# Linear attention in an adaptive transformer block: the query side token-major, scaled in place and turned by DMA

## The chip, the cores and the metric

One Trainium2 chip, one core. The time is that of one execution on the device in microseconds, the median of three runs: 209.04 us before (208.19 to 209.4). The profiled execution of the same kernel spans 207.3 us from its first to its last instruction; times read from the profile count from its start. The granted TensorE clock is 1.000 over the whole span.

The engines are called PE (TensorE: matmuls, with PEld for its weight loads), DVE (VectorE), ACT (ScalarE), POOL (GpSimd) and SP (SyncE, which only issues transfers here). Each runs its own instructions in program order; semaphores order them between engines.

## The reference

Sequence 2,048 tokens, width 512, 32 heads of 16, hidden width 1,376, all in bfloat16. Cut to what matters:

```python
mod = (silu(c) @ w_mod)            # six rows of 512: sa, ca, ga, sb, cb, gb
h = layernorm(x) * (1 + ca) + sa
q, k, v = heads(h @ wqkv)          # 32 heads of 16
pq = q @ w_phi[head]; pk = k @ w_phi[head]
phi_q = concat([softmax(pq), softmax(-pq)])   # 32 features a head, no causal mask
phi_k = concat([softmax(pk), softmax(-pk)])
kv  = sum over tokens of phi_k x v            # 32 x 16 a head
z   = sum over tokens of phi_k                # 32 a head
o   = (phi_q @ kv) / (phi_q @ z + 1e-6)
x = x + ga * (o @ wo)
h = layernorm(x) * (1 + cb) + sb
out = x + gb * ((silu(h @ w_gate) * (h @ w_up)) @ w_down)
```

The numerator and the denominator of `o` hold the same `phi_q`. A factor that both signs of one head's `phi_q` share cancels in the quotient.

## The kernel before

Tokens are worked in 16 tiles of 128 (four chunks of four). The program is written as a list of operations with the buffers that each reads and writes. Some have more than one engine to choose from. A fixed list, `ORDER`, says in which order they are placed and on which engine, and a small timing model inside the kernel only decides which buffer each gets, how instructions are interleaved, and where TensorE would idle. There it puts matmuls of ones whose result nobody reads ("fillers", line 1046).

The key side, once for each token tile; `Wk2` is the key weight with `w_phi` folded in:

```python
def k_tile(i):
    # PE: pk = hT^T Wk2, v = hT^T Wv, four matmuls of 512 columns each
    # ACT: e = exp(+pk), exp(-pk)           (128 x 1024)
    # DVE: S = sum of e over 16 features    (64 sums a token)
    # DVE or ACT: R = 1 / S
    # POOL: phik = e * R
    # ACT or DVE: va = v, with a column of ones
def kv_tile(i):     # PE: 8 matmuls of 65 columns: kv_ps += phik^T va, for four heads and both signs each
    ...
```

The query side is feature-major: 128 features by 512 tokens. It keeps the bare exponentials of both signs and normalizes later:

```python
def q_front(c_i, j):
    for k in range(KD):
        nc.tensor.matmul(pq()[:], lhsT=Wq2[:, k, j * P:(j + 1) * P], rhs=hT[c_i][k][:], ...)
    for sg in range(2):
        nc.scalar.activation(eTs[c_i, sg, j][:], pq()[:], ACT.Exp, scale=(1.0 if sg == 0 else -1.0))
```

The attention of a tile takes eight matmuls, one for eight heads of one sign, with 128 + 16 columns: numerators, the sums of the exponentials, and the products with z. DVE then joins the signs:

```python
NDW = P + 16
def attend(n):
    nd = Buf("four", lambda slot: four_ps[0])          # four banks of PSUM, one buffer
    for j in range(KD):
        for sg in range(2):
            nc.tensor.matmul(nd()[:, j, sg * NDW:(sg + 1) * NDW], lhsT=eTs[c_i, sg, j][:, ts_],
                             rhs=KVZ[:, sg * KD + j, :], start=True, stop=True)
    # ACT or DVE: Ssw[sg] = sums of the other sign          (two copies)
    # DVE: U = (products with z) * Ssw ; den = U(+) + U(-) ; den = 1 / den
    # DVE: A[sg] = sums of the other sign / den             (two products)
    # DVE: o2[sg] = numerators[sg] * A[sg]                  (two products of 128 x 512)

def turn(n, on_pe):
    if on_pe:      # tiles 0 and 1: PE, 8 matmuls against the identity add the signs and turn; ACT copies
        ...
    else:          # POOL adds the two signs, a DMA transpose on SP turns the sum
        pl.op("POOL", ..., fn=lambda: nc.gpsimd.tensor_tensor(o()[:], o2()[:, 0]..., o2()[:, 1]..., op=ALU.add))
        pl.op("XBAR", ..., fn=lambda: nc.sync.dma_start(oT()[:], o()[:], transpose=True))
```

After it come `project` (four matmuls with `wo`, the residual, the statistics of the second normalization), the transposes of the normalized tile, and the feed-forward part: gate and up (`ffn_gu`, line 906), its last 96 features (`ffn_tail`, line 948), and down (line 978). The mask that places KV for the attention:

```python
for sg in range(2):
    for r in range(2):
        # DVE: KVZ block = kv_ps block * mask (64 partitions) ; KVZ z columns = (z + eps/2) * mask
```

First loads, all on one queue but the first two: x tiles 0 and 1 (256 KB), 2 and 3 (256), key weights (2 x 256), the first 1,024 columns of `w_mod` (4 x 256), value weights (512), x 4 to 7 (2 x 256), query weights (512), the rest of x (2 x 512). `w_phi` (16 KB) and `c` go on ACT's queue.

Of the kernel before, what the change touches and what calls it, by code (L numbers as in the profile page):

```python
# [30 lines left out]
NDW = P + 16  # L31
HG = 4 * DH
UNITS = [(0, 0, 1), (0, 1, 1), (0, 2, 1), (0, 3, 1), (1, 0, 2), (1, 2, 2), (2, 0, 2), (2, 2, 2), (3, 0, 2), (3, 2, 2)]


def fm_size(m):
# [4 lines left out]
QUOTA = {'q': 9, 'turn': 9, 'T': 9, 'T2': 9, 'wo': 9, 'down': 9, 'gu': 9, 'kv': 9, 'fold': 9}  # L41
# [4 lines left out]
EARLY = ("kv", "q", "fold", "T")  # L46
# [3 lines left out]
    28, 36, 0, 12, 76, 124, 4, 32, 16, 40, 8, 304, 316, 328, 340, 128, 60, 352, 80, 132, 136, 108, 92, 44, 48, 97, 64, 84, 356, 156, 160, 112, 68,  # L50
    116, 164, 168, 56, 73, 140, 144, 53, 176, 184, 172, 181, 120, 153, 150, 20, 24, 100, 105, 89, 216, 208, 220, 264, 212, 225, 256, 200, 192, 268,
    188, 452, 360, 444, 204, 260, 196, 472, 480, 364, 456, 376, 512, 273, 368, 228, 404, 276, 396, 388, 234, 412, 392, 448, 400, 408, 416, 476, 237,
    381, 504, 488, 282, 286, 288, 372, 484, 248, 240, 308, 420, 384, 424, 516, 252, 245, 636, 438, 430, 434, 320, 500, 332, 584, 492, 496, 508, 336,
    324, 312, 640, 460, 465, 520, 628, 592, 524, 612, 620, 616, 344, 348, 632, 624, 468, 680, 672, 596, 536, 528, 296, 293, 301, 588, 441, 540, 644,
    648, 548, 676, 544, 600, 604, 688, 532, 661, 654, 658, 666, 608, 685, 560, 704, 668, 700, 812, 692, 768, 732, 736, 740, 744, 708, 720, 976, 980,
    772, 776, 780, 804, 984, 988, 761, 749, 757, 712, 696, 753, 808, 817, 764, 884, 568, 724, 888, 916, 564, 717, 820, 892, 728, 832, 912, 948, 920,
    784, 824, 828, 900, 904, 1005, 997, 952, 908, 1001, 993, 1008, 1012, 1032, 1036, 924, 956, 932, 572, 936, 940, 897, 944, 1112, 960, 1144, 1176,
    1028, 1016, 1020, 964, 968, 928, 1060, 972, 1116, 1048, 1052, 1056, 1128, 1132, 1136, 556, 1024, 1140, 1040, 1216, 1180, 1148, 1192, 1196, 1200,
    1160, 1208, 1164, 1168, 1044, 576, 1212, 1240, 1244, 580, 1152, 1120, 1172, 1124, 788, 1184, 1224, 1228, 1157, 1204, 1236, 848, 1220, 1189, 1232,
    1304, 1308, 1316, 1312, 1324, 792, 796, 552, 856, 800, 1248, 1288, 1276, 1320, 1300, 852, 860, 1280, 1328, 868, 864, 1348, 1353, 1356, 1360, 1364,  # L60
    1368, 1372, 1076, 1252, 1084, 1100, 1284, 1080, 1292, 1104, 1256, 1088, 1520, 1296, 1376, 1525, 1528, 1532, 1536, 1540, 1544, 1260, 1108, 1264,
    1064, 1380, 1384, 1388, 1392, 1396, 1092, 1268, 1096, 1072, 1272, 1068, 872, 1688, 1692, 1332, 1548, 836, 1552, 880, 1400, 1696, 1700, 1556, 1406,
    1704, 844, 1708, 1712, 1416, 876, 840, 1420, 1408, 1860, 1413, 1428, 1464, 1716, 1560, 1864, 1564, 1424, 1868, 1568, 1872, 1432, 1876, 1436, 1880,
    1472, 1572, 1884, 1720, 1444, 1452, 1460, 1448, 1577, 1468, 1476, 1888, 1892, 1440, 1724, 1580, 2060, 1456, 1585, 1480, 2064, 1728, 2068, 2072,
    1732, 2076, 2080, 1496, 1736, 1588, 1500, 1484, 1592, 1488, 1628, 1636, 1612, 1740, 1746, 2084, 1748, 1492, 2032, 1620, 1648, 1596, 1652, 1504,
    2036, 2120, 1600, 2040, 2044, 1656, 2048, 1604, 2052, 1508, 1632, 1896, 2056, 1900, 1904, 1766, 1754, 1762, 2124, 1616, 1660, 2344, 2088, 1640,
    1757, 2128, 1800, 1804, 2348, 2352, 1908, 2356, 1512, 1516, 2132, 2360, 1624, 2364, 2092, 1912, 1918, 1920, 1812, 1784, 1792, 1608, 2368, 1644,
    1788, 1768, 1772, 1664, 2136, 2140, 1808, 1933, 1929, 1925, 2372, 1776, 1796, 2377, 2380, 2384, 1668, 2096, 1820, 1828, 1836, 2144, 1816, 1340,
    2388, 2392, 2396, 1672, 2400, 2100, 2104, 1824, 1937, 2149, 1780, 2432, 2108, 1832, 1840, 2656, 2661, 1956, 1964, 1940, 2664, 1676, 2404, 2112,
    2436, 2156, 1844, 2117, 1944, 1972, 1976, 2668, 2672, 2676, 1848, 1984, 2440, 1980, 1948, 2680, 2152, 2161, 2173, 1336, 2712, 2444, 2408, 1992,  # L70
    1960, 1952, 2170, 2166, 2000, 2684, 2192, 2412, 2448, 1988, 1968, 2208, 1996, 2716, 2008, 2196, 2688, 2416, 2452, 2200, 2692, 2420, 2696, 2424,
    2456, 2004, 2700, 2720, 2012, 2016, 2176, 2704, 2708, 2724, 2020, 2728, 2216, 2180, 2744, 2748, 2968, 2430, 2972, 2976, 2980, 2024, 2984, 2224,
    2732, 2461, 2204, 2736, 2988, 2184, 2228, 2236, 2464, 2244, 2264, 2212, 2252, 2232, 2992, 2188, 2468, 2240, 2996, 1852, 3024, 2260, 2272, 2268,
    2276, 2482, 2742, 2752, 2220, 3001, 3004, 3008, 3012, 3016, 2248, 2284, 2280, 2473, 2485, 2756, 3020, 2760, 3028, 2256, 2764, 2478, 3280, 3284,
    3288, 3292, 3296, 2288, 2296, 2292, 1856, 2320, 2488, 2324, 2328, 2776, 2504, 3300, 2768, 3056, 3060, 2300, 2304, 2773, 2492, 2028, 2496, 2508,
    3304, 3336, 3308, 3312, 2520, 2528, 2780, 2500, 2332, 2308, 3316, 2512, 3320, 3064, 3324, 3328, 3332, 2576, 2536, 2540, 3592, 3340, 3368, 2548,
    3068, 3072, 3076, 3080, 2544, 2552, 2556, 3032, 2786, 3597, 2797, 2584, 2794, 2564, 3600, 3604, 3608, 3612, 3036, 2336, 2790, 2572, 2560, 2592,
    2600, 3040, 2568, 2596, 3344, 3616, 2580, 3372, 3044, 2604, 3376, 3048, 3648, 1680, 3620, 2884, 3348, 3380, 2892, 2588, 2800, 2524, 3625, 3628,
    2532, 3352, 3632, 1684, 3652, 3086, 2832, 2836, 2804, 2888, 3356, 2808, 3092, 2812, 3384, 3636, 3052, 2840, 2896, 2900, 2312, 3088, 2516, 3640,
    2844, 2816, 2852, 3644, 2316, 2340, 2904, 2820, 2824, 2632, 2860, 2828, 3098, 2608, 2636, 3388, 3680, 3684, 3656, 3660, 3664, 3668, 2640, 2612,  # L80
    2616, 2620, 3109, 2912, 3105, 2848, 2856, 2868, 2908, 2644, 2872, 3688, 3672, 3677, 2876, 1345, 2916, 2864, 3360, 2880, 2944, 2948, 3692, 3696,
    3700, 2624, 3102, 3112, 3116, 3120, 3392, 2648, 3128, 3132, 3136, 3712, 3140, 2952, 2920, 3160, 3365, 3397, 3404, 2956, 3704, 3200, 2924, 3208,
    3709, 2961, 2964, 3124, 3400, 3180, 2928, 2932, 3168, 3188, 3144, 3184, 3164, 3216, 3172, 3192, 3152, 3224, 3148, 3220, 3228, 3422, 3196, 3716,
    3733, 3721, 3726, 3730, 3804, 3176, 3768, 2652, 2628, 3417, 3413, 3408, 3156, 3256, 3812, 3204, 3424, 3492, 3428, 3776, 3212, 3260, 3264, 3232,
    3500, 3752, 3432, 3808, 3236, 3268, 3756, 3760, 3764, 3736, 3740, 3744, 3788, 3240, 3816, 3784, 3512, 3244, 3440, 3792, 3520, 3436, 2936, 3796,
    2940, 3748, 3248, 3800, 3444, 3772, 3780, 3448, 3272, 3456, 3252, 3452, 3276, 3844, 3464, 3840, 3460, 3848, 3468, 3852, 3824, 3472, 3480, 3820,
    3476, 3528, 3832, 3828, 3836, 3484, 3856, 3880, 3536, 3884, 3496, 3504, 3488, 3508, 3888, 3892, 3516, 3524, 3860, 3864, 3532, 3544, 3896, 3900,
    3540, 3868, 3548, 3552, 3568, 3572, 3576, 3872, 3876, 3556, 3560, 3564, 3904, 3908, 3912, 3580, 3585, 3588, 3916, 3920,
# [27 lines left out]


class Op:
    def __init__(self, n, alts, preds, news, at):
        self.n, self.alts, self.preds, self.news, self.at = n, alts, preds, news, at  # L120
        self.end = None


class Plan:


    HOP = {"PE": 0.32, "DVE": 0.3, "ACT": 0.24, "POOL": 0.21, "SP": 0.0, "XBAR": 1.8, "NONE": 0.0}
    OWN = {"PE": 0.0, "DVE": 0.19, "ACT": 0.19, "POOL": 0.12, "SP": 0.0, "XBAR": 0.0, "NONE": 0.0}

    def __init__(self, slots, quota):  # L130
        self.ops = []
        self.slots, self.quota = slots, quota

    def op(self, alts, r=(), w=(), us=None, fn=None):
        if isinstance(alts, str):
            alts = [(alts, us, fn)]
        preds, news, at = set(), [], 0.0
        for b in r:
            preds.update(b.writers)
            at = max(at, b.at)  # L140
# [16 lines left out]
    def room(self, b, live):  # L157

        best = None
        for i in range(self.slots[b.tag]):  # L160
            if b.tag == "one" and not (b.kind == f"last{i - 4}" if str(b.kind)[:4] == "last" else i < 4 or b.kind in EARLY):
                continue
# [4 lines left out]
        if best is not None and b.kind in self.quota:  # L167
            busy = [x for x in live[b.tag].values() if x.kind == b.kind]
            over = len(busy) - self.quota[b.kind] + 1
            if over > 0:  # L170
                ends = [x.free_at() for x in busy]
                done = sorted(e for e in ends if e is not None)
                if len(done) < over:
                    return None
# [911 lines left out]
```

The softmax here doesn't subtract the row's maximum and nothing guards it: scores larger than these inputs give would overflow.

## Time and profile before

| | before |
|---|---|
| time, median of 3 | 209.04 us (208.19 to 209.4) |
| span of the profile | 207.3 us |
| first value projection on TensorE (line 617) | 13.36 us |
| last `kv_tile` ends | 56.7 us |
| first attention (line 781) | 59.32 us |
| first tail and gate/up matmuls (lines 948, 906) | 72.0 and 72.5 us |
| last matmul group (line 978) begins | 198.3 us |
| TensorE: attention, 128 matmuls of 144 columns | 16 groups of 0.50 us |
| DVE: reduce of a key tile, 128 x 1024 to 128 x 64 | 1,194 ns, 16 times |
| DVE: `o2`, 128 x 512 from PSUM | 683 ns, 32 times |
| POOL: add of the two signs | 1,154 ns, 14 times |
| SP: DMA transposes of 128 x 512 | 40, landing 2.4 us after issue |

A row of the profile's groups says line, engine, operation, output <- inputs, shapes, count, then busy time, mean time of one in ns, and the idle time before them with what ended it. The start of one matmul to the start of the next is shorter than its recorded length, as matmuls overlap; so the lengths on the chain are used for the pitch, not the means of the groups. The window tables give the busy time of each engine in a stretch of the span.

### The profile page before, as it was taken

How to read it: one execution, taken by the hardware profiler on the slowest of the kernel's cores; microseconds unless marked ns; L12 is line 12 of the kernel's file. 1: busy time of each engine (PE TensorE's matmuls, PEld its weight loads, DVE VectorE, ACT ScalarE, POOL GpSimd, SP SyncE). 2: the span in 40 equal slices, each digit the busy share in tenths (PEclk: the TensorE clock that was granted, in tenths of full speed). 3: DMA queues.
4: the chain of work that ended last, by engine and by line, in shares of the span. 5: the costliest groups of instructions: out<-in, count | busy, mean ns of one | idle time of the engine just before them, and what ended most of it. 6: DMA issues, size and time to landing. Idle time of an engine off the chain costs nothing.

```text
span 207.3 us, 4949 instructions
## 1 busy us (share of the span) xinstructions
PE 202.4 (98%) x1876; PEld 140.0 (68%) x1876; DVE 143.1 (69%) x351; ACT 114.0 (55%) x244; POOL 131.0 (63%) x172
## 2 busy tenths in 40 slices
PE   7999999999999999999999999999999999999994
PEld 2764656454555698785887876879675787698752
DVE  6699899999676886999789687887467222322232
ACT  2689999998789974335452542422532564044300
POOL 1069999899991546689678793677749254061451
PEclk9999999999999999999999999999999999999999
DMA  5996993797000011231611233202321330020012
GB/s 176 335 389 119 321 191 87 275 406 254 4 0 0 3 25 36 51 81 26 91 32 28 58 83 81 57 0 60 79 62 28 79 85 3 13 66 27 0 34 68
DMA packets 34025, 19.76 MB, mean 95 GB/s; under 512 B 25073, under 2 KB 30674, under 8 KB 34002
## 3 DMA queue, kind: packets, MB, share of 16 engines
q1 hardware_dynamic: 33712, 19.38, 33.5%
q8 instruction: 14, 0.23, 0.5%
q10 hardware_dynamic: 290, 0.08, 0.2%
q14 instruction: 9, 0.07, 0.1%
HBM read 11.58 MB, written 2.10 MB: 66 GB/s over the span
## 4 chain that ended last, share of the span: by engine, by line
PE 92%; DMA 2%; ACT 1%; POOL 1%; DVE 1%; SPq 0%; issue 0%; DVEq 0%
PE one_ps L906 34%; PE one_ps L978 18%; PE one_ps L852 7%; PE one_ps L613 6%; PE one_ps L673 6%; PE one_ps L617 5%; PE four_ps L781 4%; PE one_ps L948 3%; PE kv_ps L1046 2%; DMA wqkv_sb<-in_A_wqkv_dram 2%; PE kv_ps L649 2%; PE one_ps L447 1%; PE one_ps L551 1%; PE one_ps L540 1%; ACT e L624 1%; POOL phik L642 1%
## 5 line engine op out<-in xcount | busy, mean ns | idle before, releaser
L978 PE MATMUL one_ps<-wd_sb,gu 128*128 128x512 bf16 (+2 forms) x176 | 41.0, 372 | 0.0
L906 PE MATMUL one_ps<-hT,wg_sb 128*128 128x256 bf16 (+1 forms) x400 | 41.0, 251 | 0.0
L906 PE MATMUL one_ps<-hT,wu_sb 128*128 128x256 bf16 (+1 forms) x400 | 40.9, 251 | 0.0
L913 ACT ACTIVATE sg<-one_ps 128x512 bf16<-128x512 f32 (+1 forms) x42 | 23.7, 576 | 27.6 <-PE one_ps L906 26.4
L906 PEld LDWEIGHTS <-wg_sb 128*128 128x128 bf16 x400 | 32.7, 98 | 4.8
L906 PEld LDWEIGHTS <-wu_sb 128*128 128x128 bf16 x400 | 32.9, 98 | 4.2
L916 DVE TENSOR_TENSOR gu<-one_ps,sg 128x512 bf16<-128x512 f32 (+1 forms) x26 | 16.6, 640 | 22.1 <-PE one_ps L906 12.8
L642 POOL TENSOR_TENSOR phik<-e,R 128x1024 bf16<-128x1024 bf16 x16 | 30.5, 1930 | 1.1 <-ACT eT L679 0.7
L922 POOL TENSOR_TENSOR gu<-usb,sg 128x512 bf16<-128x512 bf16 x16 | 18.5, 1155 | 16.8 <-ACT sg L913 13.3
L978 PEld LDWEIGHTS <-gu 128*128 128x128 bf16 (+1 forms) x187 | 17.7, 98 | 15.0
L384 DVE BATCH_NORM_STATS2 st<-x_c 128x6 f32<-128x512 bf16 x32 | 21.3, 682 | 1.4 <-DMA x_c<-in_A_x_dram 1.1
L994 POOL TENSOR_TENSOR ot<-x_c,fg 128x512 bf16<-128x512 bf16 (+1 forms) x14 | 15.7, 1118 | 8.8 <-DVE fg L990 8.8
L839 POOL TENSOR_TENSOR o<-o 128x512 bf16<-128x512 bf16 x14 | 16.1, 1154 | 7.6 <-DVE o L819 7.1
L819 DVE TENSOR_TENSOR o<-four_ps,A 128x512 bf16<-128x512 f32 x32 | 20.5, 683 | 0.0
L634 DVE TENSOR_REDUCE S<-e 128x64 f32<-128x1024 bf16 x16 | 19.0, 1194 | 0.6 <-ACT e L624 0.4
L624 ACT ACTIVATE e<-one_ps 128x512 bf16<-128x512 f32 x32 | 17.7, 631 | 1.6 <-POOL phik L642 1.0
L990 DVE TENSOR_TENSOR fg<-one_ps,gab 128x512 bf16<-128x512 f32 (+1 forms) x16 | 10.7, 672 | 11.5 <-PE one_ps L978 10.8
L679 ACT ACTIVATE eT<-one_ps 128x512 bf16<-128x512 f32 x32 | 17.5, 628 | 1.4 <-PE one_ps L673 1.3
L920 ACT CAST usb<-one_ps 128x512 bf16<-128x512 f32 x16 | 9.3, 586 | 16.3 <-PE one_ps L906 14.4
L852 PE MATMUL one_ps<-wo_sb,oT 128*128 128x512 bf16 x64 | 16.1, 379 | 0.0
L617 PE MATMUL one_ps<-wqkv_sb,hT 128*128 128x512 bf16 x64 | 15.9, 379 | 0.1
L673 PE MATMUL one_ps<-hT,Wq 128*128 128x512 bf16 x64 | 15.6, 379 | 0.1
(117 smaller groups left out, 311.2 us busy)
## 6 DMA issues: line engine op xcount, KB each, us to landing
wmod_sb<-in_w_mod_dram SPq DMA_DIRECT2D x2, 1024.0 KB, 7.0
out_dram<-ot SPq DMA_DIRECT2D x15, 128.0 KB, 2.0
wg_sb<-in_B_w_gate_dram SPq DMA_DIRECT2D x1, 1376.0 KB, 8.3
wu_sb<-in_B_w_up_dram SPq DMA_DIRECT2D x1, 1376.0 KB, 11.3
wd_sb<-in_B_w_down_dram SPq DMA_DIRECT2D x1, 1280.0 KB, 14.4
x_c<-in_A_x_dram SPq DMA_DIRECT2D x4, 256.0 KB, 4.7
wmod_sb<-in_w_mod_dram SPq DMA_DIRECT2D x4, 256.0 KB, 5.7
wqkv_sb<-in_A_wqkv_dram SPq DMA_DIRECT2D x2, 512.0 KB, 7.1
```

Of the source, the lines that this page charges most:

```text
L384: pl.op("DVE", r=reads, w=[st6], us=0.6, fn=lambda: nc.vector.bn_stats(st6()[:], src))
L617: nc.tensor.matmul(v()[:], lhsT=hT[c_i][k][:, cols], rhs=wqkv_sb[:, k, 2 * D:3 * D], start=(k == 0), stop=(k == KD - 1))
L624: nc.scalar.activation(e()[:, :, sg].rearrange("p g h f -> p g (h f)"), pk()[:].rearrange("p (g n) -> p g n", g=G), ACT.Exp, scale=(1.0, - ...
L634: pl.op("DVE", r=[e], w=[Ss], us=1.14, fn=lambda: nc.vector.tensor_reduce(Ss()[:], e()[:].rearrange("p g s h f -> p (g s h) f"), axis=AX.X ...
L642: pl.op("POOL", r=[e, R], w=[bphik[i]], us=1.92, fn=lambda: nc.gpsimd.tensor_tensor(bphik[i]()[:].rearrange("p g s h f -> p (g s h) f"), e ...
L673: nc.tensor.matmul(pq()[:], lhsT=Wq2[:, k, j * P:(j + 1) * P], rhs=hT[c_i][k][:], start=(k == 0), stop=(k == KD - 1))
L819: nc.vector.tensor_tensor(o2()[:, sg].rearrange("p j (h d) -> p j h d", d=DH), ndv()[:, :, sg, 0:P].rearrange("p j (h d) -> p j h d", d=DH ...
L852: nc.tensor.matmul(a()[:], lhsT=oT()[:, j, :], rhs=wo_sb[:, j, :], start=(j == 0), stop=(j == KD - 1))
L906: nc.tensor.matmul(ps_()[0:fsz, q * n:(q + 1) * n], lhsT=wt[:, k, m * P:m * P + fsz], rhs=h2[k], start=(k == 0), stop=(k == KD - 1))
L913: pl.op("ACT", r=[g, btab], w=[sg], us=0.08 + 0.41 * L / CW, fn=lambda: nc.scalar.activation(sg()[0:fsz, 0:L], g()[0:fsz, 0:L], ACT.Silu))
L922: pl.op("POOL", r=[usb, sg], w=[gu], us=0.17 + 0.98 * L / CW, fn=lambda: nc.gpsimd.tensor_tensor(gu()[0:fsz, 0:L], usb()[0:fsz, 0:L], sg() ...
L978: nc.tensor.matmul(fp()[:], lhsT=b()[0:fsz, c0:c0 + P], rhs=wd_[0:fsz, m, wcs], start=(m == 0), stop=(m == FM - 1))
```

## The change

The query side is made as the key side already was, token-major, and both signs of four heads lie together in 128 columns. Of the two exponentials only the negative one is scaled, by S(+)/S(-), in place. The factor S(+) that is left is common to both signs of a head and cancels in `o`. The tile is then turned by two DMA transposes, so that one matmul contracts over four heads and both signs and gives 64 numerators and 4 denominators. What is removed: the products for the sums, the joining of the two signs, and the four-bank PSUM buffer, which leaves six single banks for the whole program instead of four in its later part.

Cut to its core (cuts marked `...`):

```diff
-NDW = P + 16
 HG = 4 * DH
+NDW = HG + 4
 ...
-    def q_front(c_i, j):
+    def q_tile(n):
+        c_i, t = divmod(n, TPC)
+        eq = eqs[n]
         pq = bank("q")
-                nc.tensor.matmul(pq()[:], lhsT=Wq2[:, k, j * P:(j + 1) * P], rhs=hT[c_i][k][:], ...)
+                nc.tensor.matmul(pq()[:], lhsT=hT[c_i][k][:, cols], rhs=Wq2[:, k, :], ...)
         for sg in range(2):
-            ... nc.scalar.activation(eTs[c_i, sg, j][:], pq()[:], ACT.Exp, scale=+-1)
+            ... nc.scalar.activation(eq[:, :, sg]..., pq()[:]..., ACT.Exp, scale=(1.0, -1.0)[sg])
+        pl.op("DVE", ...: tensor_reduce(Sq, eq, axis=AX.X, op=ALU.add))          # 128 x 1024 -> 128 x 64
+        pl.op("DVE", ...: reciprocal(Rq, Sq[:, :, 1]))
+        pl.op([("DVE", ...), ("POOL", ...)]: Rq = Rq * Sq[:, :, 0])
+        pl.op([("POOL", ...), ("DVE", ...)]: eq[:, :, 1] = eq[:, :, 1] * Rq)      # 128 x 512
+        for h in range(2):
+            pl.op("XBAR", ...: nc.sync.dma_start(pT()[:, h * KD:(h + 1) * KD, :], eq[:, h * KD:(h + 1) * KD]..., transpose=True))
 ...
     def attend(n):
-        nd = Buf("four", lambda slot: four_ps[0])
+        nd = Buf("four", lambda slot: kv_ps)
-            ... matmul(nd()[:, j, sg * NDW:(sg + 1) * NDW], lhsT=eTs[c_i, sg, j][:, ts_], rhs=KVZ[:, sg * KD + j, :])
-        ... Ssw, U, den, reciprocal, A, two products for o2
+            for g in range(G):
+                nc.tensor.matmul(ndv()[:, g, 0:NDW], lhsT=pT()[:, g, :], rhs=KVZ[:, g, :], start=True, stop=True)
+        pl.op("DVE", ...: reciprocal(A()[:], ndv()[:, :, HG:NDW]))
+        pl.op("DVE", ...: o = ndv()[:, :, 0:HG] * A)                              # 128 x 512
 ...
     def turn(n, on_pe):
-            ... 8 matmuls against the identity add the signs and turn
+            ... 4 transposes
-            pl.op("POOL", ...: o = o2[0] + o2[1])
             pl.op("XBAR", ...: nc.sync.dma_start(oT()[:], o()[:], transpose=True))
 ...
-    for sg in range(2): for r in range(2): two masking instructions on 64 partitions
+    one masking instruction for the numerators and one for z, on 128 partitions
 ...
     def ffn_tail: gate and up weights lie in one tile, wgu_sb[:, k, 2, F]
-            8 matmuls of 96 columns
+            4 matmuls of 2 x 96 columns
```

The first loads in their new order, all on SP's queue except `c`: x tiles 0 and 1 (256 KB), key weights (512, one transfer), `w_phi` (16), the first columns of `w_mod` (2 x 512), x 2 and 3 (256), value weights (512), x 4 to 7 (512), query weights (512). The rest of x is loaded where the order puts it. `ORDER` is new as a whole, so other operations too have changed their engine and place: of the 16 value tiles DVE copies 1 instead of 6, ACT makes 7 of the 16 reciprocals of the key sums instead of 2, and of the late outputs POOL adds 3 instead of 14. The durations in the inner timing model are changed as well, and the rules about which PSUM bank may serve what are gone.

## The prediction

> **What bounds the kernel now.** I read the page from the top: busy shares, then the forty slices, then the chain that ended last.
>
> ```profile
> PE 202.4 (98%) x1876; PEld 140.0 (68%) x1876; DVE 143.1 (69%) x351; ACT 114.0 (55%) x244; POOL 131.0 (63%) x172
> ...
> PE   7999999999999999999999999999999999999994
> PEld 2764656454555698785887876879675787698752
> DVE  6699899999676886999789687887467222322232
> ACT  2689999998789974335452542422532564044300
> POOL 1069999899991546689678793677749254061451
> ...
> PE 92%; DMA 2%; ACT 1%; POOL 1%; DVE 1%; SPq 0%; issue 0%; DVEq 0%
> ```
>
> TensorE is busy in all but the first and last slices and is 92% of the chain. But in slices 3 to 11 (some 10 to 57 us) DVE, ACT and POOL stand at 8 or 9 as well: while the key side is made, four engines are near full. Afterwards the other three have room. "Busy" doesn't say that TensorE does useful work, so the next view is the chain in order of time, which gives the pitch of each kind of matmul, and the waits of TensorE.
>
> ```profile
> 12.84 0.52 PE kv_ps L1046 x3
> 13.36 0.86 PE one_ps L617 x4
> ...
> 43.44 0.26 PE kv_ps L649 x8
> ...
> 56.73 0.86 PE one_ps L692 x4
> 57.59 1.73 PE one_ps L673 x8
> 59.32 0.50 PE four_ps L781 x8
> ...
> 63.77 0.45 PE one_ps L834 x8
> ...
> 92.01 0.34 PE one_ps L948 x8
> ```
>
> The columns are start, length, what, and how many. Four 512-column matmuls take 0.86 us (215 ns each), eight of 65 columns 0.26, the attention of a tile (eight of 144) 0.50, its turn 0.45, eight tail matmuls of 96 columns 0.34. TensorE hardly waits in the waits view (0.2 us for a weight load, 1.4 us at the very start); where it would have waited, the program has put filler matmuls of ones (L1046). They are the hidden idle time: 16,471 columns in the program, 6.9 us at 215 ns per 512. About 3.7 us of them stand before the first value projection at 13.36 us, 3.1 us after it.
>
> Then the load by stage (columns: stretch, its length, busy us and instructions of PE, PEld, DVE, ACT, POOL, then clock, DMA share, GB/s):
>
> ```profile
> 13.00:57.00 44.00, 43.82 (x375) 23.85 (x372) 39.92 (x74) 40.48 (x82) 40.91 (x32) 1.00 0.73 217
> 57.00:130.00 73.00, 72.99 (x771) 53.19 (x770) 59.59 (x174) 39.84 (x95) 49.31 (x69) 1.00 0.21 43
> 130.00:203.00 73.00, 73.00 (x601) 54.40 (x599) 32.85 (x74) 26.60 (x53) 38.08 (x51) 1.00 0.16 42
> ```
>
> In the key stage DVE, ACT and POOL have only 3 to 4 us of slack in 44. After 57 us they have 13 to 40 us. So a cut of TensorE work counts in full after 57 us, as long as its inputs arrive, and before that only if no other engine is pushed over its 44 us.
>
> **What the Trainium skill says.** "Perfetto Trace Analysis", section "Identifying the Most-Contended Engine", warns that matmul busy time is a poor measure; hence the pitches and fillers above, and the trace agrees: 98% holds 6.9 us of fillers. "TensorE: Matmul & The Clock Gate", section "Back-to-back issue gap", gives columns / 2.4 + 2.5 ns: 216 ns for 512, 62.5 ns for 144, 29.6 ns for 65; measured 215, 62.5 and 32.5. The same section's 81 ns for 128 columns in a stream with weight loads is not seen here: four turns of 128 columns take 0.22 us, 55 ns each. "VectorE: DVE Perf Modes", section "The perf-mode tier table", says a reduce, and a two-tensor operation with PSUM, run one element per cycle; the rows agree (1,194 ns for the reduce of 1,024 elements, 683 ns for 512 from PSUM), so the new reduce can't be expected to be cheap.
>
> **The change part by part, TensorE first.**
> - Attention: eight matmuls of 144 columns become eight of 68. The nearest row is 65 columns, 0.26 us for eight; with 68 I take 0.265. Saved 16 x (0.50 - 0.265) = 3.8 us.
> - Turns of the first two tiles on TensorE: 8 matmuls become 4, 0.45 to 0.22 us; 2 x 0.23 = 0.5 us.
> - Tail: eight of 96 columns become four of 192. At 192/512 x 215 ns = 81 ns, four take 0.32 against 0.34; 16 x 0.02 = 0.3 us.
> - Projections, keys, values, gate, up and down keep their number and columns. The query projection keeps 64 of 512 with the operands exchanged.
>
> That is 4.6 us of work gone, spread from 59 us on, where TensorE sets the end.
> - Fillers: the instruction order of the changed program has 9,456 columns of them, 3.9 us. Before its first value projection 3.4 us stay; after it 3.1 us become 0.5, so 2.6 us are taken away. This is no work saved: it is gained only if the waits they covered are gone. Part is: query tiles can be projected one at a time from 128 tokens and are placed between the key tiles. I credit 1.7 of the 2.6.
> - First loads: before, x (512 KB), key weights (512) and the first modulation columns (1,024) come ahead of the first modulated tile; now x 256, keys 512, 16, modulation 1,024. 240 KB less, at the 335 to 389 GB/s of the second and third slice, is 0.6 to 0.7 us. The value weights land no earlier (2,576 KB in the queue against 2,560), but at those rates they are in by about 11.5 us and aren't the wait. In DVE's new order two statistics of late tiles (682 ns each) stand ahead of the first modulated tile, so I credit 0.5.
>
> Sum: 4.6 + 1.7 + 0.5 = 6.8 us.
>
> **The other engines.** Added per query tile: reduce 1.19 us and reciprocal 0.35 on DVE, a product (about 0.18, the row of A) and a scaling of 512 elements (estimate 0.68 on DVE, 1.15 on POOL, from rows of that size), and two DMA transposes. Removed per tile: copies of sums (about 0.37 where on DVE), U 0.22, den 0.22, A 0.37 and one of the two 0.68 products on DVE; and the add of 1.15 us on POOL in 14 tiles. So over the whole kernel DVE and POOL come out about level, but the work moves forward in time. In the order, only four of the sixteen reduces stand ahead of the masking of KV. Key stage, DVE: + 4 x (1.19 + 0.35), + 3 x 0.18, + 3 x 0.68, + 5 tiles of modulated x at 0.4 = + 10.7; taken off: 5 value casts (0.66), 5 reciprocals (0.55), a key-fold cast (0.68) and 1.5 us of masking = - 8.2. Net + 2.5 on 39.9: still under 44. ACT gets 5 value casts (0.61), 5 Ln/Exp pairs (0.55), 3 key-fold casts (0.59) and some more query exponentials, and loses 5 modulations (0.84): + 3.4 to + 5 on 40.5. That is full. POOL loses 3 normalizations (0.77) and the clearing of KV (1.2), and gains two power pairs (0.95): about 1.5 us less. I expect ACT and TensorE to share the bound, and the key stage to end about where it ended, with three more query tiles projected by then.
>
> The chain of one attention gets shorter: before, from the first attention at 59.32 to its turn at 63.77 takes 4.5 us; after, matmul, reciprocal and one product, 0.27 + 0.35 + 0.68 and handovers, under 2 us.
>
> SyncE: 32 transposes more. Before, one takes 1.21 us of issue and lands 2.4 us after it. From the first query tile's transposes to the last there are 55 in the order, 55 x 1.25 = 69 us, in a stretch that I put at 46 to 125 us: 87% full and in order, so one late tile can hold the next. I take 0.
>
> Then 209.0 - 6.8 = 202.2; as the shorter attention chain leaves some slack I say **202.0 us** (3.4% less).
>
> **The rivals.**
> 1. ACT and DVE become the bound of the key stage. For it: 40.5 and 39.9 us of 44 before, and the sums above; buffers of three key tiles. Against: three more query tiles are there to fill TensorE. Costs 1 to 3 us: 203 to 205.
> 2. SyncE's queue becomes the wait: attention held for its turned query tile, and with it the down-stream tiles. For it: 87% full, in order, 2.4 us to land. Against: the first four tiles are made early, and the queue's waits in the page before are for producers, not for room. Costs 1 to 4 us: 203 to 206.
> 3. The fillers were real waits and stay as idle time: 2.6 us credited at 0 gives 203.7; fully credited with a start 0.7 us earlier, 201.1.
> 4. The old attention chain, four banks of one buffer, kept TensorE waiting more than the fillers show, so that the gain is larger: below 200.5. Against: the pitches after 72 us leave no gap.
>
> **Range and chances.** The work removed, 4.6 us, is by itself over the 4.2 us that make 2%; fillers and start add up to 3.3; new waits may take back 1 to 4. 199.5 to 205.5 holds it 8 in 10. Faster by over 2% (below 204.9): 0.84; within: 0.14; slower: 0.02, for a queue that blocks badly.
>
> **What would show it.** In the profile after: attention 0.26 to 0.27 us for eight; the tail 0.32 for four; the first value projection at 12.5 to 13.1; the last key/value accumulation within 1 us of 56.5; first gate/up near 68.5 against 72.5; the end of the chain TensorE again, 200 us of span. Wrong step by step: idle TensorE released by ACT or DVE between 13 and 57 us (rival 1), by transposed query tiles between 60 and 130 us (rival 2). It would be wrong as a whole if TensorE's idle time exceeded 3 us after 13 us.

## The result, and the profile after

The changed kernel takes 216.12 us (median of 4, 215.22 to 216.96) against 209.22 us for the kernel before beside it: a ratio of 1.0347 (95% interval 1.0308 to 1.0386), slower by 3.5%. Its profiled execution spans 213.3 us.

The page of the changed kernel, lines that answer to those shown of before (busy shares, two rows of the forty slices, the chain that ended last by engine):

```profile
PE 195.6 (92%) x1748; PEld 131.0 (61%) x1771; DVE 153.4 (72%) x301; ACT 113.5 (53%) x237; POOL 114.5 (54%) x162
...
PE   7899998996978999699999899999989999899993
...
DVE  6689999999999997779897686868566202433243
...
PE 42%; DVE 22%; DMA 20%; POOL 5%; SPq 4%; issue 4%; ACT 2%; DVEq 0%; POOLq 0%; ACTq 0%
```

TensorE was 92% of the chain before and is 42% now; DVE and transfers have 22% and 20%, against 1% and 2%. DVE stands at 9 from slice 4 to slice 15, without a gap. The chain in order of time shows that the new work itself costs what it should (start, length, what, how many):

```profile
66.53 0.26 PE kv_ps L768 x8
...
68.51 0.22 PE one_ps L786 x4
...
75.09 0.33 PE one_ps L894 x4
```

An attention takes 0.26 us for eight (0.50 before), a turn 0.22 (0.45), the tail 0.33 for four. The time went into waits. TensorE's two largest waits in the stretch from 10 us on (what waited, for whom, total us, times, longest):

```profile
PE kv_ps L768 <- DMA pT<-eq: 3.7, 4, 1.7
PE kv_ps L768 <- DVE KVZ L742: 1.4, 1, 1.4
```

Over the whole span TensorE's waits come to 13 us, against 1.6 before. They have two main places. The windows by stage (stretch, length, busy us and instructions of PE, PEld, DVE, ACT, POOL, clock, DMA share, GB/s):

```profile
13.00:57.00 44.00, 40.48 (x324) 20.79 (x329) 42.88 (x74) 39.10 (x85) 35.15 (x27) 1.00 0.77 217
57.00:130.00 73.00, 66.48 (x733) 48.52 (x741) 62.71 (x124) 39.88 (x87) 51.41 (x80) 1.00 0.46 81
```

TensorE lost 3.3 us of busy time in the first stretch and 6.5 in the second, compared with before. The key stage now runs past the first stretch: the first value projection comes at 11.54 us (13.36 before), but the masking of KV only at 62.5 (56.8 before), the first attention at 63.3 (59.3) and the first gate/up at 74.5 (72.5). Not all of the 5.7 us is lost: by the masking TensorE has done 36 matmuls of the query projection, and 24 before. These 12 are three query tiles, 2.6 us at 215 ns each, and need not be done later.

DVE around the masking:

```profile
58.90 2.20 DVE L664 TENSOR_TENSOR eq<-eq,Rq 128x512 bf16<-128x512 bf16 x1
61.03 1.21 DVE L656 TENSOR_REDUCE Sq<-eq 128x64 f32<-128x1024 bf16 x1
62.27 0.35 DVE L658 RECIPROCAL Rq<-Sq 128x32 f32<-128x32 f32 x1
62.54 0.13 DVE L740 SCALAR_TENSOR_TENSOR KVZ<-kv_ps,bm4z 128x32 bf16<-128x32 f32 x1
```

The row of POOL's timeline that ends in this stretch:

```profile
56.74 3.82 POOL L618 TENSOR_TENSOR phik<-e,R 128x1024 bf16<-128x1024 bf16 x2 [0.27 <-PE one_ps L648]
```

The last accumulation of KV began at 60.61 and took about 0.26; the masking (L740) stood on DVE behind a scaling, a reduce and a reciprocal of query tiles, and TensorE waited 1.4 us for it. The larger part of the delay lies earlier: the accumulation itself came some 4 us later than before. And the scaling lasted 2.20 us, three times the 0.68 that the prediction took for it: it ended 0.54 us after POOL's product (L618), which ended at 56.74 + 3.82 = 60.56. The rows of the three kinds of DVE operation in question up to 62.5 us (after the bar: busy us, mean ns of one; busy time counts overlaps once):

```profile
L558 DVE TENSOR_SCALAR hT<-raw,modA 128x512 bf16<-128x512 bf16 x5 | 5.0, 1058 | 0.2 <-DMA raw<-xn 0.2
...
L664 DVE TENSOR_TENSOR eq<-eq,Rq 128x512 bf16<-128x512 bf16 x2 | 3.8, 1922 | 0.0
...
L659 DVE TENSOR_TENSOR Rq<-Rq,Sq 128x32 f32<-128x32 f32 x2 | 1.5, 772 | 0.0
```

These are the modulations of x (L558), the scalings (L664) and the small products (L659). Their means are longer than the 0.4, 0.68 and 0.18 us that the prediction took.

The other place is SyncE. Its queue between 91 and 102 us:

```profile
91.67 1.20 SPq L815 DMA_TRANSPOSE raw<-xn  x1
92.98 2.64 SPq L670 DMA_TRANSPOSE pT<-eq  x2
95.73 1.21 SPq L790 DMA_TRANSPOSE oT<-o  x1
97.03 2.62 SPq L815 DMA_TRANSPOSE raw<-xn  x2
99.75 2.52 SPq L670 DMA_TRANSPOSE pT<-eq  x2
```

Eight transposes fill 10.2 of the 10.6 us. The queue has almost no room here, and it works in order, so a tile that comes late makes those behind it late.

### The profile page after: what moved, and what is told of

It reads as the page before. It is cut to its first block, busy times and chain, and to the rows that moved or that the text cites. A ratio compares the mean times of both kernels' runs of the same rounds, so it can differ in the third digit from the quotient of the medians.

```text
span 213.3 us, 4651 instructions
## 1 busy us (share of the span) xinstructions
PE 195.6 (92%) x1748; PEld 131.0 (61%) x1771; DVE 153.4 (72%) x301; ACT 113.5 (53%) x237; POOL 114.5 (54%) x162
## 3 DMA queue, kind: packets, MB, share of 16 engines
q1 hardware_dynamic: 51072, 23.59, 45.8%
## 4 chain that ended last, share of the span: by engine, by line
PE 42%; DVE 22%; DMA 20%; POOL 5%; SPq 4%; issue 4%; ACT 2%; DVEq 0%; POOLq 0%; ACTq 0%
PE one_ps L853 21%; PE one_ps L924 11%; DMA pT<-eq 7%; DVE S L610 6%; DMA raw<-xn 5%; DMA wq<-in_A_wqkv_dram 4%; PE one_ps L799 4%; DVE Sq L656 3%; PE one_ps L648 3%; DVE hT L558 2%; DVE eq L664 2%; DMA out_dram<-ot 2%; SPq L282 2%; DMA WT<-wq 2%; PE kv_ps L768 1%
## 5 line engine op out<-in xcount | busy, mean ns | idle before, releaser
L853 PE MATMUL one_ps<-hT,wgu_sb 128*128 128x256 bf16 (+1 forms) x800 | 76.1, 251 | 0.8 <-DVE fg L936 0.8
L853 PEld LDWEIGHTS <-wgu_sb 128*128 128x128 bf16 x800 | 65.2, 98 | 10.4 <-issue 0.9
L618 POOL TENSOR_TENSOR phik<-e,R 128x1024 bf16<-128x1024 bf16 x16 | 31.1, 1958 | 6.8 <-DVE R L616 3.4
L656 DVE TENSOR_REDUCE Sq<-eq 128x64 f32<-128x1024 bf16 x16 | 19.2, 1201 | 0.0
L802 DVE TENSOR_TENSOR x_c<-x_c,one_ps 128x512 bf16<-128x512 bf16 x16 | 10.9, 684 | 9.9 <-PE one_ps L799 9.9
L652 ACT ACTIVATE eq<-one_ps 128x512 bf16<-128x512 f32 x32 | 17.1, 623 | 0.6 <-PE one_ps L648 0.6
L593 PE MATMUL one_ps<-wv,hT 128*128 128x512 bf16 x63 | 15.9, 379 | 1.7 <-ACT e L600 1.0
L824 ACT ACTIVATE hT<-raw,modB 128x256 bf16<-128x256 bf16 (+1 forms) x17 | 8.8, 568 | 14.0 <-DMA raw<-xn 14.0
L589 PE MATMUL one_ps<-wk,hT 128*128 128x512 bf16 x59 | 15.7, 379 | 0.2
L648 PE MATMUL one_ps<-wq,hT 128*128 128x512 bf16 x63 | 15.7, 379 | 0.1
L826 POOL TENSOR_SCALAR hT<-raw,modB 128x256 bf16<-128x256 bf16 (+1 forms) x12 | 6.1, 520 | 12.5 <-DMA raw<-xn 12.5
## 6 DMA issues: line engine op xcount, KB each, us to landing
x_c<-in_A_x_dram SPq DMA_DIRECT2D x3, 512.0 KB, 10.6
```

The source lines that it names most:

```text
L618: pl.op("POOL", r=[e, R], w=[bphik[i]], us=1.92, fn=lambda: nc.gpsimd.tensor_tensor(bphik[i]()[:].rearrange("p g s h f -> p (g s h) f"), e ...
L648: nc.tensor.matmul(pq()[:], lhsT=hT[c_i][k][:, cols], rhs=Wq2[:, k, :], start=(k == 0), stop=(k == KD - 1))
L652: pl.op("ACT", r=[pq, btab], w=[be[sg]], us=0.48, fn=lambda sg=sg: nc.scalar.activation(eq[:, :, sg].rearrange("p g h f -> p g (h f)"), pq ...
L656: pl.op("DVE", r=be, w=[Sq], us=1.14, fn=lambda: nc.vector.tensor_reduce(Sq()[:].rearrange("p g s h -> p (g s h)"), eq[:].rearrange("p g s ...
L853: nc.tensor.matmul(ps_()[0:fsz, q * n:(q + 1) * n], lhsT=wgu_sb[:, k, i, m * P:m * P + fsz], rhs=h2[k], start=(k == 0), stop=(k == KD - 1))
```

## The experiments

Two theories for the loss. **Queue**: SyncE's queue of transposes holds the turned query tiles. **Key stage**: more work, and work held up, stands ahead of the masking of KV. In the key stage two causes rival: DVE held by POOL, or the sum of work on DVE, ACT and POOL. The kernel before took 208.2 us beside these runs; each ratio is to it. Except in the new orders, the order of the instructions is that of the changed kernel.

### DVE's held work moved; one transpose; both

```diff
 # e1_ports: five modulations on ACT, five scalings and products of query tiles on POOL
-("DVE*", 0.3, lambda j=j: nc.vector.tensor_scalar(hT[c_i][j]..., raw..., modA..., modA...))
+("DVE*", 0.3, lambda j=j: nc.scalar.activation(hT[c_i][j]..., raw..., ACT.Identity, bias=..., scale=...))
-("DVE", 0.12, lambda: nc.vector.tensor_tensor(Rq...))   ("DVE", 0.62, lambda: fm(nc.vector))
+("DVE", 0.12, lambda: nc.gpsimd.tensor_tensor(Rq...))   ("DVE", 0.62, lambda: fm(nc.gpsimd))
 # e2_onedma: one transpose of 128 x 1024 for a query tile
-for h in range(2): nc.sync.dma_start(pT()[:, h * KD:(h + 1) * KD, :], eq[:, h * KD:(h + 1) * KD]..., transpose=True)
+nc.sync.dma_start(pT()[:], eq[:]..., transpose=True)
 # e3_both: the two together
```

> The changed kernel with its order untouched, but the five modulations of the first norm that stood on DVE run on ACT, and the products and scalings of the query tiles that stood on DVE (five of each) run on POOL. Theory A (DVE instructions with two SBUF inputs or a fast one-input form are held until POOL's running product ends: 2.1 to 2.2 us instead of 0.4 to 0.7): the masking of KV begins near 58 us instead of 62.5, and the time falls by 2 to 4 us, to 212 to 214. Rival B (DVE is simply over-full with the new reduces and reciprocals): the masking moves by less than 1.5 us and the time stays within 1 us of 216.

> The changed kernel with one DMA transpose of 128 x 1024 for each query tile in place of two of 128 x 512. Theory C (SyncE's queue is full from about 70 to 130 us because each transpose takes 1.2 us of it whatever its size): 16 instructions fewer, some 20 us less on the queue, attention no longer waits for turned query tiles, the time falls by 3 to 5 us, to 211 to 213; the key stage is unchanged. Rival D (the queue's time goes with the bytes, or the tiles come late because their scaling is late): one transpose takes about 2.4 us, and the time stays within 1 us of 216.

> Both edits. If A and C hold and are separate losses, the gains add up: 6 to 8 us, 208 to 210. If one queue only waits because the key stage is late, the sum is no better than the larger of the two.

Measured: e1 216.7 us, ratio 1.0366 (1.0300 to 1.0432); e2 210.54, 1.0105 (1.0067 to 1.0143); e3 209.73, 1.0063 (1.0041 to 1.0085).

The queue's share is thus 216.1 - 210.5 = 5.6 us. The changed kernel itself was measured only beside a kernel before of 209.2 us, not 208.2; taken from the ratios, 1.0347 - 1.0105, the share is 5.0 us. The instructions of the turned tile `pT` in the changed kernel, the row of its transposes (duration in ns min/median/max, first and last start):

```profile
L670 SPq DMA_TRANSPOSE pT<-eq x32: 1188/1222/2138, 52.7 to 135.4; - x32
```

The same row in e2:

```profile
L668 SPq DMA_TRANSPOSE pT<-eq x16: 1231/1237/2157, 54.0 to 129.4; - x16
```

Twice the size at the same 1.2 us of the queue: sixteen of them are saved, and TensorE's wait for turned query tiles (3.7 us in four waits) is gone in e2.

Freeing DVE alone gave nothing (e1; its 216.7 us is what rival B gave), and with the queue relieved only 0.8 us (e2 to e3); e3's time is in its expected range, but almost all of the gain is e2's. In e1 DVE's busy time from 13 to 57 us fell from 42.88 to 37.21 us, but ACT's rose from 39.10 to 41.46, and the masking came at 62.0 instead of 62.5. So neither "DVE was held" nor "DVE is over-full" is by itself the cause of the late key stage.

### The cost of single instructions

This kernel has none of the block's computation. It runs DVE's operations four times alone and four times beside a chain of POOL products of 128 x 1024 (the first modulation of these ended before POOL began), and four transposes of each size on SyncE.

> Not the computation: only single instructions of the forms in dispute are run, and the output is a copy of x. On DVE, four of each form first with POOL idle, then again beside 24 products of 128 x 1024 on POOL that follow each other: the modulation (one SBUF input, 512 bf16), the scaling of 512 by a broadcast and the small product (both with two SBUF inputs), the reduce of 1,024, the reciprocal of 32, a product with one input from PSUM, a copy from PSUM. Theory A: beside POOL the first three last up to one POOL product longer (some 1.9 us more at most), the other four as alone. Rival: all are slowed alike, or none. Then DMA transposes on SyncE of 128, 512, 1,024 and 2,048 columns, four each. Theory C: each takes 1.2 to 1.3 us of the queue whatever its size, while landing grows; rival D: the queue's time doubles from 512 to 1,024.

The timeline (start, length, instruction), the second of four alone and the second of four beside POOL, whose products stand in one row of eight:

```profile
7.78 0.41 DVE L43 TENSOR_SCALAR mod1alone<-x,sc 128x512 bf16<-128x512 bf16 x1
8.10 0.69 DVE L45 TENSOR_TENSOR scl1alone<-x,sc 128x512 bf16<-128x512 bf16 x1
8.70 0.18 DVE L48 TENSOR_TENSOR prd1alone<-sc 128x32 f32<-128x32 f32 x1
...
20.88 16.10 POOL L67 TENSOR_TENSOR pool<-x,sc 128x1024 bf16<-128x1024 bf16 x8
...
25.75 1.42 DVE L43 TENSOR_SCALAR mod1beside<-x,sc 128x512 bf16<-128x512 bf16 x1
27.09 2.41 DVE L45 TENSOR_TENSOR scl1beside<-x,sc 128x512 bf16<-128x512 bf16 x1
29.42 1.91 DVE L48 TENSOR_TENSOR prd1beside<-sc 128x32 f32<-128x32 f32 x1
...
31.25 1.21 DVE L50 TENSOR_REDUCE red1beside<-x 128x64 f32<-128x1024 bf16 x1
```

A modulation goes from 0.41 to 1.42 us, a scaling from 0.69 to 2.41, a tiny product from 0.18 to 1.91; the reduce (1.21), the reciprocal (0.34), and what reads PSUM (0.62 and 0.67) stay as they are. POOL's eight products take 2.01 us each, so they end at 26.92, 28.93 and 30.94 us; the three held operations end 0.25, 0.57 and 0.39 us after one of these. So each waits for the product that is running and ends 0.2 to 0.6 us later.

The 1.42, 2.41 and 1.91 us agree with the Trainium skill, "SBUF — State Buffer", section "Who interferes with whom". It says that DVE's two-port fast modes contend with GpSimd for a pair of ports that they share, and the one that comes second "fully blocks" for the whole of the other's instruction; and that a DVE operation with two SBUF inputs contends with a GpSimd instruction that reads SBUF. "GPSIMD Engine Reference", section "1. Specifications", names the same two kinds in a row of its table.

The same kernel's SyncE queue, four transposes of 128, 512, 1,024 and 2,048 columns:

```profile
4.13 4.99 SPq L77 DMA_TRANSPOSE turn128x<-x  x4
...
9.16 5.20 SPq L79 DMA_TRANSPOSE turn512x<-x  x4
...
14.41 5.45 SPq L79 DMA_TRANSPOSE turn1024x<-x  x4
...
19.91 9.96 SPq L79 DMA_TRANSPOSE turn2048x<-x  x4
```

1.25, 1.30, 1.36 and 2.49 us each: up to 1,024 columns the queue is charged by the instruction, hardly by the byte.

### Normalization of the query tiles left out: all, and only the first four

```diff
 # e4_nonorm (two transposes) and e7_nonorm_onedma (one): reduce, reciprocal, product, scaling left out for all 16 query tiles
 # e12_nonorm4 (one transpose): left out for tiles 0 to 3 only
-fn=lambda: nc.vector.tensor_reduce(Sq()[:]..., eq[:]..., axis=AX.X, op=ALU.add))
+fn=lambda: None if n < 4 else nc.vector.tensor_reduce(Sq()[:]..., eq[:]..., axis=AX.X, op=ALU.add))
 # likewise the other three
```

> The changed kernel with the whole scaling of the query tiles left out (no reduce, no reciprocal, no product, no scaling; the exponentials are turned as they are), so what is computed is no longer the reference. It frees DVE of 16 x 1.2 + 16 x 0.35 us and of the held scalings, and POOL of 11 x 1.06 us. Theory A: the five modulations stay held (about 3 us), so the masking of KV comes at 56 to 57 us and the time falls by 4 to 6 us, to 210 to 212, the rest being SyncE's queue. Rival B: masking at 53 to 54 us; with a queue that is no limit the time falls to 206 or less.

> Reduce, reciprocal, product and scaling of the query tiles left out (the output is then not normalized on the query side), and one transpose a tile instead of two; order untouched. Without the normalizations alone it was 211.8 us, with one transpose alone 210.5, the changed kernel 216.1. Theory (two separate losses, the work in the key stage and the queue of transposes, that add up): 211.8 - 5.6 = 206 to 207.5, masking at 59.6, no wait of TensorE for turned query tiles. Rival (after the removal of one loss the other one is hidden by the same slack): 209 to 211.

> The kernel with one transpose a tile (210.5 us), and the normalization (reduce, reciprocal, product, scaling) left out for the first four query tiles only, whose reduces stand ahead of the masking of KV on DVE; the other twelve keep theirs, order untouched, so four tiles of the output are not normalized on the query side. Theory (the loss is made before the masking, where the sum of DVE, ACT and POOL decides; after it there is room): as with all sixteen left out, masking near 59.6 and 205.5 to 206.8 us. Rival (the normalization costs all along the kernel): three quarters of the gain of 4.7 us stay away, 208.8 to 210.

Measured: e4 211.82 us, ratio 1.0151 (1.0105 to 1.0197); e7 205.87, 0.9887 (0.9871 to 0.9904); e12 206.16, 0.9898 (0.9883 to 0.9912). e7 and e12 came out as their theories said. e4's time is theory A's, but its masking, at 59.6 us, came later than theory A or rival B had it.

The two losses add up: 4.3 us for the normalization with two transposes, 4.7 with one. And of the 4.7 us, the four tiles ahead of the masking carry 4.4; the other twelve, three quarters of the work, cost 0.3. This places the loss: before the masking, not after it. Ahead of the masking the four tiles take 11.5 us of DVE in e2: 6.2 of reduces and reciprocals, which are not held, and 5.3 of scalings and products, of which 3.5 are hold. DVE in e12 (in brackets: idle time before, and what ended it):

```profile
60.09 0.19 DVE L739 SCALAR_TENSOR_TENSOR KVZ<-kv_ps,bm4z 128x32 bf16<-128x32 f32 x1 [3.74 <-PE kv_ps L625]
```

The masking now waits for TensorE, not for DVE's queue.

### Which engine ends the key stage

All of these have one transpose a tile.

```diff
 # e5_pool: e3, with the five modulations on POOL instead of ACT
+("DVE*", 0.3, lambda j=j: nc.gpsimd.tensor_scalar(hT[c_i][j]..., raw..., modA..., modA..., op0=ALU.mult, op1=ALU.add))
 # e9_va_dve: e5, with five value copies on DVE (e11_va8: eight of them)
-("ACT", 0.48, lambda: fva(nc.scalar.copy))
+("ACT", 0.48, lambda: fva(nc.vector.tensor_copy if i in (5, 7, 9, 11, 13) else nc.scalar.copy))
 # e13_wo_dve: e9, with the four products that scale wo on DVE
 # e10_swap: e2, with the five modulations on ACT and the five value copies on DVE
```

> As the run with one transpose and ports freed (209.73 us), but the five modulated tiles are made on POOL instead of ACT; order untouched. Theory (the key stage of the changed kernel lost its time to DVE held by POOL; moved to ACT, the five instructions of 0.84 us filled the next engine, so the gain of freeing DVE did not show): the masking of KV comes 1 to 2.5 us earlier than 62.3, and the time is 207 to 209. Rival (the key stage is bounded by the order and by arrivals, not by the load of any one engine): masking stays at 62 to 63.5 us and the time within 1 us of 209.7; POOL's five extra instructions of about 1 us could even delay its own products and put it over 211.

> The kernel with one transpose, scalings and modulations on POOL (207.6 us), and the value copies of key tiles 5, 7, 9, 11 and 13 go from ACT to DVE; order untouched. ACT loses 5 x 0.61 = 3 us of its 44.9 in 48.5, DVE gains 5 x 0.66 = 3.3 on 41.1; they read PSUM and so are not held by POOL. Theory (ACT, over-full, ends the key stage): masking at 58 to 59 instead of 59.9, time 205.5 to 207. Rival (POOL, 44.6 us of 48.5, or arrivals end it now): masking within 0.5 us of 59.9 and 207.2 to 208.2.

> As the run with five value copies on DVE, but eight (tiles 4 to 7, 9 to 11, 13): ACT loses 4.9 us, DVE gains 5.3 and would stand near 46 of 48.5. Theory: no better than with five, 206 to 208, as DVE becomes the full engine in turn. Rival (ACT is still the bound with five): a further 0.5 us or more off, to 205 to 206.

> The kernel with one transpose a tile (210.5 us), and a swap: DVE's five modulations (held by POOL, 0.41 us unheld) go to ACT (0.84 us), and five value copies (from PSUM, not held) go from ACT (0.61) to DVE (0.66). By unheld durations both engines get more work: DVE + 1.3 us, ACT + 1.2 us. Theory (the hold is what costs, not the work): DVE's busy time to the mask falls by about 1.5 to 2 us (five held modulations took 5.0 us), masking 1 us or more earlier than 63.8, time 208.5 to 210. Rival (the plain work is what costs): masking later than 63.8, time 211 or more.

> The kernel with one transpose, scalings and modulations on POOL and five value copies on DVE (207.64 us), and the four products that scale wo (1.16 us each on POOL, just after the masking) go to DVE; order untouched. In that run TensorE waited 0.7 us for them and the pitch showed 1.1 us of loss about them at 62 to 66 us. Theory (POOL, after it took the scalings, ends the next stretch): 206.3 to 207.2. Rival (the transposed query tiles or the DVE chain come out next): 207.4 to 208.

Measured: e5 207.61 us, ratio 0.9982 (0.9959 to 1.0004); e9 207.64, 0.9970 (0.9959 to 0.9980); e11 208.13, 0.9990 (0.9981 to 1.0000); e13 207.77, 0.9979 (0.9961 to 0.9997); e10 210.11, 1.0077 (1.0047 to 1.0107).

e5 is as the theory said: the same five instructions, taken from full ACT to POOL, which had the most room, bring 2.1 us, and the masking 2.4 us earlier (59.9). After that nothing helps: five copies off ACT gave no change, eight slightly worse. The window of e5 from its first value projection to its masking suggests why (columns as above):

```profile
11.50:60.00 48.50, 45.52 (x375) 23.50 (x374) 41.05 (x74) 44.92 (x98) 44.61 (x38) 1.00 0.74 210
```

TensorE is at 94%, ACT at 93%, POOL at 92%, DVE at 85%: no engine that could be relieved stands out. So e9 and e13 came out as their rivals said, and e11 0.1 us above what its theory gave. e10 was to weigh hold against plain work. DVE's busy time to the masking fell by 1.9 us (57.4 to 55.5), where unheld durations would have it rise by 1.3, so the hold is at work there; but time and masking (63.8 in both) stayed, with DVE's two held scalings still ahead of it. Its time, 210.11 us, lies between the two expectations and settles nothing. The profiles of e2, e11 and e13 had a granted clock of 0.95 to 0.97 up to the masking, all others 1.00, so the maskings of these three are only rough.

### New orders

```diff
-ORDER = [...]      # of the changed kernel
+ORDER = [...]      # e6_reorder, e8_reorder2: from a search over a timing model that holds DVE while POOL runs
+                   # e14_order_pool: the same with held durations charged to DVE, which moves most of that work to POOL
```

> One transpose a tile, and a new instruction order, searched with DVE's two-input and fast instructions held while POOL runs, and with the measured 1.33 us a transpose on the queue; the operations themselves are those of the changed kernel. Theory (the change is worth what was predicted, and the two costs left out of the order's timing ate it): 201 to 205, under the kernel before. Rival (the key stage of the changed kernel needs its 5 us more in any order, since the query work has moved into it): 208 to 211, no better than the old order with one transpose.

> A second order from the same search with another seed, operations the same. Theory: within 1.5 us of the first new order, 201 to 205. Rival: the two orders differ by more than 3 us, so an order's gain is luck with handovers rather than the two costs.

> One transpose, and a new order searched with DVE's held instructions charged at their held durations, which puts most scalings, products and modulations on POOL. Theory (load and holds are what matters, and an order that knows them loses less): 204.5 to 207, under the run with five value copies on DVE. Rival (the key stage needs the sum of its work on three engines, in any order): 207 to 210.

Measured: e6 209.74 us, ratio 1.0080 (1.0063 to 1.0097); e8 210.52, 1.0110 (1.0094 to 1.0126); e14 210.65, 1.0122 (1.0102 to 1.0143). The theory that a better order would bring the predicted time fell: none beats the old order with the same single transpose by more than 0.8 us, and in e6 and e14 the masking comes at 62.6 all the same. e6 lies in its rival's range, e8 within 1.5 us of e6 as expected but not at 201 to 205, and e14 above both of its expectations. It doesn't show that no order could do better.

### What the runs say together

Busy time of the three vector engines from the start to the masking of KV, from the window tables:

| | masking at | DVE + ACT + POOL | share of three engines | time |
|---|---|---|---|---|
| before | 56.8 us | 48.9 + 47.5 + 43.4 = 139.7 us | 82% | 209.2 us |
| after | 62.5 | 57.1 + 51.8 + 44.0 = 152.9 | 82% | 216.1 |
| e3, both | 62.3 | 50.0 + 53.8 + 43.6 = 147.4 | 79% | 209.7 |
| e5, POOL | 59.9 | 48.6 + 50.6 + 47.1 = 146.3 | 81% | 207.6 |
| e12, four tiles not normalized | 60.1 | 48.1 + 50.3 + 42.1 = 140.5 | 78% | 206.2 |
| e6, new order | 62.6 | 56.5 + 53.3 + 45.8 = 155.6 | 83% | 209.7 |

In none of the sixteen kernels, those outside the table included, do the three reach more than 83% together, and in none less than 78%. From before to after the sum grew by 13.2 us; a third of that at 82% is 5.4 us, and the masking came 5.7 us later. But this is loose, and the runs do not show that the sum alone decides: e12 has the sum of before (140.5 and 139.7 us) and its masking comes 3.3 us later, and from e3 to e5 the sum fell by 1.1 us, worth some 0.5 of stage, while the masking came 2.4 us earlier. Between 78% and 83% lie some 4 us of a stage of 60. So the sum serves as a first estimate; how it is spread, and what waits for what, decides the rest.

## Why the prediction was wrong

- **TensorE work removed (4.6 us): right.** Attention 0.26, turns 0.22, tail 0.33, within 0.01 us of what was taken.
- **First loads (0.5 us): too small.** The first value projection came 1.8 us earlier than before, at 11.54 us and not at 12.5 to 13.1. It brought nothing to the end of the key stage, since that does not end on TensorE.
- **The DVE sum of the key stage (+ 2.5 us): the first step that failed.** To the masking DVE's busy time rose by 8.2 us. The terms that were mis-sized: five modulations, taken at 0.4 us each, had a mean of 1,058 ns (5.0 us instead of 2.0); three scalings at 0.68, two in fact, of 1,922 ns (3.8 instead of 2.0); three products at 0.18, two in fact, of 772 ns (1.5 instead of 0.5). Together 5.8 us. The lengths 0.18 and 0.68 came from rows of before that read PSUM, which the run m1 shows is not held, and 0.4 is about the unheld length (0.41 there); beside POOL's running products all three are held. ACT (+ 4.3 by the windows, + 3.4 to + 5 predicted) was right; POOL rose by 0.7 where 1.5 less was expected.
- **"Still under 44", "to end about where it ended": the second.** Each engine was compared with the length of the stage by itself. But three engines that hand tiles to each other were at 82% together before, and at 78 to 83% in every version. Even the predicted additions, 2.5 + 3.4 - 1.5 = 4.4 us at the least, would be an estimated 1.8 us of stage at that share. The reading of the rows was too broad as well: DVE, ACT and POOL all stand at 8 or 9 in slices 4 to 10, not 3 to 11; POOL has 6 in slice 3, DVE 6 and ACT 7 in slice 11. Rival 1 saw the place, with 1 to 3 us; the four query tiles' normalization alone cost 4.4.
- **"SyncE: I take 0": the third.** 87% full and in order is not free: 5.0 to 5.6 us. This is rival 2 (1 to 4 us), larger than its range. Against it stood that the queue waited for producers and not for room; that held for the kernel before, with 40 transposes, and not for this one.
- **Fillers (1.7 us credited).** With both losses taken out (e7, 205.9 us) 3.9 us stay over the predicted 202. TensorE's waits are 4.9 us there against 1.6 before, 3.3 more, which fits rival 3: the fillers taken away stood for real waits. That is argued from the sums, not tried, and rival 3 is worth at most the 1.7 us credited. The waits are spread over handovers from ACT, DVE, POOL and weight transfers; which of them is the cause was not settled.

The sum: 202.0, + 5.6 for the queue, + 4.7 for the normalization (4.4 of it ahead of the masking), + 3.9 not settled further, is 216.2. It closes because the last term is what was left over; measured against the kernel before of 208.2 us it would be nearer 4.7.

How much of the 4.4 us is the hold and how much plain work also stays open. Against the unheld durations DVE lost some 6.5 us ahead of the masking: 5.0 - 2.0 for the modulations, 3.8 - 1.4 for the scalings, 1.5 - 0.4 for the products. But moving that work brought only 0.8 us while it went to full ACT, and 2.9 when the modulations went to POOL.

In a better form the change about breaks even: with one transpose a tile, and modulations and scalings on POOL and value copies on DVE, it takes 207.64 us, 0.3% under the kernel before (0.2 to 0.4).

## What to carry to other kernels

When work is moved forward into a stage where several engines feed each other, add up the busy time of all of them and compare it with the share that they reached together before, as a first estimate; that each alone stays under the stage's length says little. Before a DVE operation with both inputs in SBUF, or in its fast form, is counted, ask whether POOL runs beside it: here it waited for the rest of POOL's running product, up to 1.7 us, and then took about its own length. And count a DMA transpose by the instruction on its queue: up to 1,024 columns here, turn as much at once as lies ready.

## What the runs showed of the hardware beyond that

- The hold takes no account of size: a product of 128 x 32, 0.18 us alone, took 1.91 us beside POOL's products of 2.0 us.
- The size of a transpose shows later, in its landing: in m1 those of 128, 512, 1,024 and 2,048 columns landed 2.4, 2.5, 3.4 and 4.7 us after issue, while the first three held the queue for nearly the same time.
